# Reordering the list of batch 0, turning the last x by DMA, and moving one VectorE sum in a fused hash attention and gated feed-forward kernel

## The chip, the cores and the metric

The kernel runs on one core of a Trainium2 chip. A core has five engines that run their own instruction streams: TensorE (PE, matrix products; PEld is its weight load), VectorE (DVE), ScalarE (ACT), GpSimd (POOL) and SyncE (SP, which here issues most DMA transfers). The metric is the device time of one execution in microseconds (us); lower is better. Before the change the median of 3 runs is 340.48 us (340.46 to 341.31).

## What is computed

There are 4 batches, 8 heads, 768 positions and 64 values a head. First a masked attention: each query and each key gets a bucket of 6 sign bits, and a query sees the keys of its own bucket alone.

```python
q_bits = (einsum('bhsd,dk->bhsk', q, proj) > 0)      # the same for k
mask   = q_bucket[:, :, :, None] == k_bucket[:, :, None, :]
scores = where(mask, (q @ k^T) / sqrt(D), -1e9)
x      = softmax(scores) @ v                          # heads side by side: 3072 tokens x 512
```

Then a gated feed-forward block on x, with d_ff = 1536:

```python
ffn = (gelu(x @ w_gate) * (x @ w_val)) @ w_out
out = x + sigmoid(x @ w_res) * ffn
```

## The kernel before

A pair p is two heads; a batch has 4 pairs, and p runs from 0 to 15. The bits of queries and keys stand as extra rows beside the 64 values in a tile nat (token by column; four buffers, used in turn by pairs and sides), which is turned into aug (column by token), so that one matmul gives the masked score. The scores of a pair are cut into 9 chunks, so a batch has 36 slots: `scores` (line 542) makes 1024 columns in one of two PSUM buffers sp, ScalarE takes the exponential (line 553), and `values` (line 515) multiplies it with v (in the tile va, with a column of ones) into av. `finish` (lines 466 and 467) divides and writes x_tok; x_tok is turned into x_sb either by a DMA transpose that SP issues (line 470) or on TensorE (`x_turn`, lines 497 to 504: six transposes into PSUM and copies to SBUF).

`gate_val` (lines 570 to 588) then runs 12 steps m: 8 matmuls with w_gate, 8 with w_val (line 566), the Gelu on ScalarE (line 583), and their product hh on VectorE (line 586), which gives the sp buffer of w_val back. Behind the product of step m stand the pieces that were registered for it with `gv`. The last quarter of x is multiplied last in step 0: the first 12 matmuls (`begun`) are issued ahead. `project` (lines 592 to 623) is a generator that gives one matmul at a time; the matmuls of batch b's projection are dealt out over the 36 slots of batch b+1 by `mlp_mm`, and the last HELD = 16 of the 96 are kept to cover the turning of the last x.

The program's order is written out by hand; each engine runs its instructions in that order and waits on semaphores. For batch 0 it is the list ORDER (lines 20 to 30), names of pieces that `job` defines (lines 713 to 766). sN and vN are the scores and the values of slot N. trPS (P pair, S side: 0 query, 1 key) is VectorE's transpose for the hash, hNI a quarter of a hash product on TensorE, tkN its result back to tokens, btPS the bits, csPS the cast of the values into nat on GpSimd, tpPSH and tdPSH the turning of half H on TensorE and its copy on VectorE, tuPS the turning by DMA instead. ldPS and lvP are loads on SP, vaP and vsP the tile va and the sums of v on GpSimd, wN a piece of the weights loaded from GpSimd's queue (w0, w2, w4, w6: w_gate; w1, w3, w5, w7: w_val; w8: w_res; w9 to w11: w_out), finPH a finish, xtP an x_turn, g0 and g1 the begun matmuls, op40, pr40 and rp40 the preset of pair 4's result. The lists BESIDE (lines 31 to 44) say which pieces stand behind which step of batch 0's gate_val.

For the batches behind it, the bits of two of the pairs are made without TensorE: `part` (line 357, GpSimd) multiplies the values by one row of proj, and `part_sum` (line 361, VectorE) adds up; there are 24 of each a batch, and PROD and SUMS (lines 771 and 772) say behind which step each stands (12 and up are slots of the next batch). They are planned for batches 1 and 2.

Of the kernel before, what the change touches and what calls it, by code (L numbers as in the profile page):

```python
# [18 lines left out]
X_PE = 2  # L19
ORDER = """  # L20
trq tpB tdk tdq trk s0 hoq tr10 ld50 s1 bo0 s2 ho bo1 tp001 td001 s3 tp011 td011a ld40 tr11 ld51 v0
v1 cs21 td011b s4 s5 h00 h01 h02 h03 tr20 s6 s7 v2 v3 v4 tk0 bt10 bt11 tp100 tp110 td100 td110 tr21
s8 tr30 tr31 tp111 td111 cs31 s9 tp101 td101 s10 w0 v5 v6 v7 v8 s11 cs20 s12 ld61 fin00 ld41 h10 h11
w1 s13 h12 h13 fin01 cs30 s14 lv3 ld70 s15 va1 v9 v10 v11 s16 tk1 bt20 bt21 bt31 tp200 tp210 td200
td210 vs1 s17 tp211 td211 cs41 tr50 s18 tp201 td201 va2 s19 tp310 vs2 s20 vs3 bt30 td310 v12 v13 s21
v14 fin10 s22 tp300 tr40 w2 tp301 s23 v15 tr51 s24 lv4 va4 v16 v17 s25 v18 s26 v19 v20 v21 td301
td300 s27 fin11 v22 s28 cs50 tp311 s29 ld71 v23 fin20 w3 w4 s30 lv5 w5 v24 v25 td311 s31 v26 fin21
va3 tr41 v27 s32 w6 v28 v29 v30 s33 xt2 s34 v31 s35 gelu tr61 v32 v33 v34 g0 v35 fin30 op40 g1 fin31
xt3 ld60 h20 h21 h22 w7
"""  # L30
BESIDE = [
    "vs4 lv6 cs40 h23 tk2 bt41",
    "cs51 bt50",
    "tu50 cs70 tr70",
    "bt40 tu40 cs60 w8 w9 w10 w11",
    "bt51",
    "tr71",
    "tu51",
    "tr60",
    "h30 h31 h32 tu41 cs61 h33 tk3 bt60 bt61 tu60 tu61",  # L40
    "cs71 bt71 tu71",
    "bt70 tu70",
    "pr40 rp40",
]

@with_exitstack
def kernel(
# [13 lines left out]
    B, H, S, D = q.shape  # L61
# [7 lines left out]
    HP = H // 2  # L69
# [222 lines left out]
    def stripes(ht):  # L292
        n = ht.shape[1]
        return ht.rearrange("p (a c) n -> p a c n", a=3)[:, :, 0:HT // 3] if n > HT else \
            ht.rearrange("p (a c) n -> p a c n", a=3)
# [59 lines left out]
    def part(x, j):  # L355
        pd = t32_pool.tile([P, HT, D], FP32, tag="t32", name="pd")
        nc.gpsimd.tensor_mul(pd, raw[x], prow[:, j].unsqueeze(1).to_broadcast([P, HT, D]))  # L357
        hparts[x, j] = pd

    def part_sum(x, j):  # L360
        nc.vector.tensor_reduce(stripes(hsum6)[:, :, :, j],  # L361
                                hparts.pop((x, j)).rearrange("p (a c) d -> p a c d", a=3), axis=mybir.AxisListType.X, op=ALU.add)

    def bits_sum(x):
        nc.vector.tensor_scalar(nat_of(x)[:, :, D:D + NBITS].rearrange("p (a c) n -> p a c n", a=3),
                                stripes(hsum6), 0.0, 0.5,
                                op0=ALU.is_gt, op1=ALU.subtract)

    def turn(p, side):
        x = (p, side)  # L370
        ag = aug_pool.tile([P, HT, P], BF16, tag=f"aug{side}", name=f"aug{side}")
        nc.sync.dma_start_transpose(out=ag, in_=nat_of(x).rearrange("p c n -> p (c n)"))
        aug[x] = ag
# [84 lines left out]
    def finish(p, hi):  # L458
        b, hp = divmod(p, HP)
        if hp == 0 and hi == 0:  # L460
            x_tok[b] = x_pool.tile([P, HP, T, 2 * D], BF16, tag="x_tok", name="x_tok")
            x_sb[b] = x_pool.tile([P, HP, T, P], BF16, tag="x_sb", name="x_sb")
        o = av.pop((p, hi))
        acc_done((p, hi))
        rec = sm_pool.tile([P, T], FP32, tag="rec", name="rec")
        nc.vector.reciprocal(rec, o[:, 0:T, D])
        nc.vector.tensor_mul(x_tok[b][:, hp, :, hi * D:(hi + 1) * D], o[:, 0:T, 0:D],
                             rec.unsqueeze(2).to_broadcast([P, T, D]))
        if hi == 1 and (0 < b < B - 1 or hp < HP - (X_PE if b == 0 else 1)):
            nc.sync.dma_start_transpose(out=x_sb[b][:, hp],  # L470
                                        in_=x_tok[b][:, hp].rearrange("p t n -> p (t n)"))

# [23 lines left out]
    def x_turn(b, hp):  # L496
        pt = mm_ps.tile([P, T, P], BF16, tag=take(), name="pt")
        for t in range(T):
            nc.tensor.transpose(pt[:, t, :], x_tok[b][:, hp, t, :], ident)  # L499
        if hp == HP - 1:  # L500
            nc.scalar.activation(x_sb[b][:, hp, 0:2], pt[:, 0:2], AF.Copy)
            nc.vector.tensor_copy(x_sb[b][:, hp, 2:T], pt[:, 2:T])
        else:
            nc.vector.tensor_copy(x_sb[b][:, hp], pt)
# [154 lines left out]
    NSLOT = HP * NCH  # L659
    LAST = NPAIR * NCH  # L660
    LAG = 2
    HELD = 16
    AHEAD = 3
    side_pe, side_work = {}, {}

# [103 lines left out]

    FROM = 1  # L770
    PROD = (0, 0, 0, 0, 0, 1, 2, 2, 6, 7, 8, 8, 10, 10, 10, 12, 13, 13, 13, 19, 19, 20, 22, 27)
    SUMS = (1, 2, 2, 4, 5, 6, 7, 8, 9, 10, 10, 11, 12, 12, 13, 17, 19, 21, 21, 23, 23, 29, 30, 31)
    PROD0 = (0, 1, 2, 3, 4, 5, 6, 7, 8, 9, 10, 11, 12, 14, 16, 17, 19, 20, 22, 24, 25, 27, 28, 30)
    SUMS0 = (1, 2, 3, 4, 5, 6, 7, 8, 9, 10, 11, 12, 14, 16, 18, 19, 21, 22, 24, 26, 27, 29, 30, 32)
    CASTS0 = (3, 5, 8, 10)
    CASTS = (2, 5, 10, 11)
    VALS = (9, 6)
    LAYS = (0, 0, 3, 5)
# [4 lines left out]
    for b in range(B - 1):  # L783
        s0, p0 = b * NSLOT, (b + 1) * HP
        xs = [(p0 + i, side) for i in range(2) for side in range(2)]
        ys = [(p0 + 2 + i, side) for i in range(2) for side in range(2)]
        if b > 0:
            for j, (x, y) in enumerate(zip(xs, ys)):
                at(s0 + 24 + 2 * j, lambda x=x: tr(*x))
                at(s0 + 25 + 2 * j, lambda x=x: cast(*x, nc.gpsimd))  # L790
                loads(s0 + 2 + 4 * j, (x[0], "qk"[x[1]]))
                loads(s0 + 18 + 3 * j, (y[0], "qk"[y[1]]))
            gv(b, 0, lambda p0=p0: tokens((p0, p0 + 1), True))
            for m, x in zip(LAYS, xs):
                lay(b, m, x)
            for m, y in zip(CASTS, ys):
                gv(b, m, lambda y=y: cast(*y, nc.gpsimd))
        else:
            for m, names in enumerate(BESIDE):
                for name in names.split():  # L800
                    gv(b, m, first.pop(name))
        if b >= FROM:
            s1 = s0 + NSLOT

            def put(n, piece):
                if n < 0:
                    at(s1 + n, piece)
                elif n < KF:
                    gv(b, n, piece)
                else:  # L810
                    at(s1 + n - KF, piece)

            plan, prod, sums = [], PROD if b else PROD0, SUMS if b else SUMS0
            for i, (y, j) in enumerate((y, j) for y in ys for j in range(NBITS)):
                plan.append((prod[i] + .3, lambda y=y, j=j: part(y, j)))
                plan.append((sums[i] + .2, lambda y=y, j=j: part_sum(y, j)))
                if j == NBITS - 1:
                    plan.append((sums[i] + .2, lambda y=y: (bits_sum(y), turn(*y))))
            for n, piece in sorted(plan, key=lambda e: e[0]):
                put(int(n // 1), piece)  # L820
    for p in range(HP, NPAIR):
# [6 lines left out]
    mlp, done = [], [0]  # L828
    NMM = T * (KM + KF)

    def mlp_mm(n):
        while mlp and n > 0:
            try:
                next(mlp[0])
                n -= 1
                done[0] += 1
            except StopIteration:
                mlp.pop(0)
# [6 lines left out]
    for s in range(NSLOT, LAST):  # L845
        p, c = divmod(s, NCH)
        b, slot = divmod(s, NSLOT)
        cur = scores(p, c)
        for piece in side_pe.pop(s, []):
            piece()  # L850
        mlp_mm(AHEAD + (slot + 1) * (NMM - HELD - AHEAD) // NSLOT - done[0])
        pending.append(cur)
        while len(pending) > LAG:
            values(*pending.pop(0))
        for piece in side_work.pop(s, []):
            piece()
        if slot == NSLOT - 1:
            values(*pending.pop(0))
            ps = (HP * (b + 1), HP * (b + 1) + 1)
            mlp_mm(4)  # L860
            flush()
            begun = [gv_mm(b, 0, w, 0, KM - 1) for w in (wg, wv)]
            if b < B - 1:
                mlp_mm(NMM)
                gate_val(b, begun, lambda: hashed(ps))
            else:
                x_turn(b, HP - 1)
                mlp_mm(HELD - 7)
                gv(b, 0, lambda: mlp_mm(NMM))
                gate_val(b, begun, lambda: mlp_mm(3))  # L870
            done[0] = 0
            mlp.append(project(b))
# [33 lines left out]
```

## Time and profile before

| what | value |
|---|---|
| median of 3 runs | 340.48 us |
| profiled execution | 340.31 us |
| its span, first to last instruction | 338.6 us |
| TensorE busy | 333.2 us (98%) |
| VectorE busy | 216.9 us (64%) |
| ScalarE busy | 206.2 us (61%) |
| GpSimd busy | 171.9 us (51%) |
| granted TensorE clock | 1.000 |

The list of batch 0 reaches its first gate matmuls at 44.38 us; its gate_val ends at 79.9. Each later batch then has its 36 slots and its gate_val: the first score of batch 1 stands at 79.93, that of batch 2 at 158.50, that of batch 3 at 237.07. A row of a timeline reads: start, duration, engine, line, operation, what it writes and reads, shapes, count, and in brackets the idle time of the engine just before it and what ended it. Matmuls are pipelined, so a row's duration holds the latency of the last one; the distance between the starts of two rows is what they take. SPq and POOLq rows are the issue of a DMA; its landing is a number of its own.

### The profile page before, as it was taken

To read this page: it belongs to the slowest core of one execution; us is meant where nothing else is said; L and a number is where in the kernel's file an instruction comes from. 1 tells how busy PE (TensorE), PEld (TensorE's weight loads), DVE (VectorE), ACT (ScalarE), POOL (GpSimd) and SP (SyncE) were. 2 spreads that over 40 slices of the span, in tenths; PEclk is the share of its full clock that TensorE was granted. 3 is DMA by queue.
4 is the path that set the end of the run, shared out by engine and by line. 5 is a ranking of instruction groups with operands and counts; after the bars stand their busy time and mean duration, and the time that the engine had idled before them with its cause. 6 is when DMAs were issued, how large, how long until landed. Compare 5 with 4: busy or idle time off the path is not lost.

```text
span 338.6 us, 7598 instructions
## 1 busy us (share of the span) xinstructions
PE 333.2 (98%) x3058; PEld 203.1 (60%) x3058; DVE 216.9 (64%) x418; ACT 206.2 (61%) x232; POOL 171.9 (51%) x220
## 2 busy tenths in 40 slices
PE   8999999999999999999999999999999999999995
PEld 4667766655666655655666665656566665666444
DVE  6889457574445748888887766887897444343343
ACT  4889963317999952235999982233999984223220
POOL 5879920410665306998999704998998000000000
PEclk9999999999999999999999999999999999999999
DMA  7997897799876634350488832551261420000012
GB/s 211 379 249 169 160 252 128 132 190 199 240 164 187 207 94 99 73 96 0 126 219 204 277 106 62 102 96 28 48 148 39 97 56 33 31 0 2 31 64 94
DMA packets 71459, 43.09 MB, mean 127 GB/s; under 512 B 49536, under 2 KB 68480, under 8 KB 71424
## 3 DMA queue, kind: packets, MB, share of 16 engines
q1 hardware_dynamic: 65008, 37.37, 43.7%
q0 software_dynamic: 6336, 5.24, 10.1%
q8 instruction: 24, 0.39, 0.5%
q14 instruction: 11, 0.09, 0.1%
q10 hardware_dynamic: 80, 0.00, 0.0%
HBM read 29.56 MB, written 6.29 MB: 106 GB/s over the span
## 4 chain that ended last, share of the span: by engine, by line
PE 91%; ACT 4%; DVE 3%; issue 1%; DVEq 0%; ACTq 0%
PE sp L566 35%; PE fps L614 18%; PE sp L542 17%; PE av L515 9%; PE rps L598 6%; ACT hh L553 4%; PE hs L283 2%; DVE hh L586 1%; PE wps L189 1%; PE pt L384 1%; PE hs L330 1%; DVE nat L319 1%; DVE hsum L361 0%; PE pt L499 0%; DVE o L621 0%
## 5 line engine op out<-in xcount | busy, mean ns | idle before, releaser
L553 ACT ACTIVATE e<-sp 128x1024 bf16<-128x1024 f32 x108 | 109.0, 1028 | 8.1 <-PE sp L542 2.8
L357 POOL TENSOR_TENSOR pd<-ld,prow 128x768 f32<-128x768 f32 x48 | 86.1, 1811 | 36.8 <-PE hs L283 32.6
L583 ACT ACTIVATE gt<-sp 128x768 bf16<-128x768 f32 x48 | 38.9, 810 | 89.8 <-PE sp L566 89.8
L542 PE MATMUL sp<-aug,aug 71*128 71x256 bf16 (+1 forms) x384 | 85.5, 325 | 0.1
L614 PE MATMUL fps<-wo,hh 128*128 128x512 bf16 (+2 forms) x312 | 79.5, 362 | 0.0
L566 PE MATMUL sp<-x_sb,wv 128*128 128x512 bf16 (+1 forms) x384 | 70.9, 326 | 0.4 <-DVE hh L586 0.4
L566 PE MATMUL sp<-x_sb,wg 128*128 128x512 bf16 (+1 forms) x384 | 70.9, 326 | 0.1
L586 DVE TENSOR_TENSOR hh<-gt,sp 128x768 bf16<-128x768 bf16 x48 | 45.8, 954 | 39.0 <-PE sp L566 34.2
L515 PEld LDWEIGHTS <-e 128*128 128x128 bf16 x864 | 40.2, 97 | 25.1
L566 PEld LDWEIGHTS <-wv 128*128 128x128 bf16 x384 | 37.6, 98 | 25.5 <-issue 0.8
L566 PEld LDWEIGHTS <-wg 128*128 128x128 bf16 x384 | 36.9, 98 | 25.8 <-issue 1.7
L361 DVE TENSOR_REDUCE hsum<-pd 128x12 f32<-128x768 f32 x48 | 44.4, 943 | 0.5
L515 PE MATMUL av<-va,e 128*128 128x65 bf16 x864 | 43.4, 193 | 0.0
L614 PEld LDWEIGHTS <-hh 128*128 128x128 bf16 x312 | 28.1, 97 | 21.8
L553 ACT ACTIVATE hh<-sp 128x1024 bf16<-128x1024 f32 x36 | 34.5, 1024 | 3.4 <-PE sp L542 3.0
L542 PEld LDWEIGHTS <-aug 71*128 71x128 bf16 x384 | 29.5, 97 | 11.0 <-issue 1.1
L617 DVE SCALAR_TENSOR_TENSOR fps<-th,fps 128x512 f32<-128x512 f32 (+2 forms) x26 | 16.9, 650 | 28.3 <-PE fps L614 27.8
L598 PE MATMUL rps<-wr,x_sb 128*128 128x512 bf16 x96 | 27.1, 379 | 0.0
L494 DVE COPY av<-av 128x390 f32<-128x390 f32 x24 | 13.7, 571 | 19.6 <-PE av L490 19.6
L602 ACT ACTIVATE th<-rps 128x512 f32<-128x512 f32 x24 | 14.3, 594 | 18.5 <-PE rps L598 18.5
L223 POOL TENSOR_SCALAR nat<-ld 128x768 bf16<-128x768 f32 (+1 forms) x16 | 13.0, 813 | 18.6 <-DMA aug<-nat 18.0
L265 DVE STREAM_TRANSPOSE t<-ld 128x768 f32<-128x768 f32 (+1 forms) x24 | 21.9, 925 | 0.1
(77 smaller groups left out, 259.6 us busy)
## 6 DMA issues: line engine op xcount, KB each, us to landing
ldv<-in_v_dram SPq DMA_DIRECT2D x16, 384.0 KB, 5.1
out_dram<-o SPq DMA_DIRECT2D x23, 256.0 KB, 2.0
ld<-in_q_dram SPq DMA_DIRECT2D x15, 384.0 KB, 5.6
ld<-in_k_dram SPq DMA_DIRECT2D x15, 384.0 KB, 6.0
wg<-in_moe_w_gate_dram POOLq DMA_DIRECT2D x4, 384.0 KB, 9.1
wv<-in_moe_w_val_dram POOLq DMA_DIRECT2D x4, 384.0 KB, 11.8
wo<-in_moe_w_out_dram POOLq DMA_DIRECT2D x3, 512.0 KB, 11.8
wr<-in_moe_w_res_dram POOLq DMA_DIRECT2D x1, 512.0 KB, 7.7
```

What stands on the lines that cost most here:

```text
L265: nc.vector.transpose(t32[p, side][:, sl].rearrange("p c h n -> p (c h n)"), raw[p, side][:, sl].rearrange("p c d -> p (c d)"))
L357: nc.gpsimd.tensor_mul(pd, raw[x], prow[:, j].unsqueeze(1).to_broadcast([P, HT, D]))
L361: nc.vector.tensor_reduce(stripes(hsum6)[:, :, :, j], hparts.pop((x, j)).rearrange("p (a c) d -> p a c d", a=3), axis=mybir.AxisListType.X ...
L515: nc.tensor.matmul(av[p, hi][:, qt, :], e[:, off:off + P], va[:, hi, jt, 0:D + 1], start=first, stop=(p >= HP and jt == T - 1), skip_group ...
L542: nc.tensor.matmul(sp[:, off:off + nq * P], ks[0:KA, hi * T + jt, :], qs[0:KA, hi * T + qt0:hi * T + qt0 + nq, :], start=True, stop=True)
L553: nc.scalar.activation(e, sp, AF.Exp, scale=float(ALPHA))
L566: nc.tensor.matmul(sp[:, c0:c1], w[:, kk, bass.ts(m, P)], xs[:, kk, c0:c1], start=(kk == 0), stop=(kk == KM - 1))
L583: nc.scalar.activation(gt, sp[:, 0:S], AF.Gelu)
L586: nc.vector.tensor_mul(hidden[b][:, m, :], gt, ps[1][:, 0:S])
L598: nc.tensor.matmul(rps, x_sb[b][:, kk, t, :], wr[:, kk, :], start=(kk == 0), stop=(kk == KM - 1))
L614: nc.tensor.matmul(fps[:, cs], hh[:, m, bass.ts(t, P)], wo[:, m, cs], start=(m == 0), stop=(m == KF - 1))
L617: nc.vector.scalar_tensor_tensor(fps[:, cs], th[:, cs], 1.0, fps[:, cs], op0=ALU.add, op1=ALU.mult)
```

## The change

The first 27 names of the list stand as they are. Behind them the same pieces stand in another order; some loads, casts and weight pieces move far, and some pieces change between the list and the steps of gate_val (w8 comes into the list; w6, w7 and the others stand together at its end). BESIDE is dealt out anew: w8 leaves, the hash of pairs 6 and 7 goes from step 8 to step 9, tr70 from 2 to 3, tr60 from 7 to 4.

The fifth entry of SUMS goes from 5 to 4, in batches 1 and 2. PROD0, SUMS0 and CASTS0 go; nothing read them, because the loop plans these pieces from batch 1 on.

In the last batch the fourth pair's x is turned by a DMA transpose like the others, and `x_turn` is not called there any more. Four more matmuls of the projection are held back in that batch, from slot 12 on one by one up to 20 instead of 16, and of them 10 instead of 9 stand between the begun matmuls and the last quarter of step 0.

```diff
 ORDER = """
 trq tpB tdk tdq trk s0 hoq tr10 ld50 s1 bo0 s2 ho bo1 tp001 td001 s3 tp011 td011a ld40 tr11 ld51 v0
-v1 cs21 td011b s4 s5 h00 h01 h02 h03 tr20 s6 s7 v2 v3 v4 tk0 bt10 bt11 tp100 tp110 td100 td110 tr21
-s8 tr30 tr31 tp111 td111 cs31 s9 tp101 td101 s10 w0 v5 v6 v7 v8 s11 cs20 s12 ld61 fin00 ld41 h10 h11
-w1 s13 h12 h13 fin01 cs30 s14 lv3 ld70 s15 va1 v9 v10 v11 s16 tk1 bt20 bt21 bt31 tp200 tp210 td200
-td210 vs1 s17 tp211 td211 cs41 tr50 s18 tp201 td201 va2 s19 tp310 vs2 s20 vs3 bt30 td310 v12 v13 s21
-v14 fin10 s22 tp300 tr40 w2 tp301 s23 v15 tr51 s24 lv4 va4 v16 v17 s25 v18 s26 v19 v20 v21 td301
-td300 s27 fin11 v22 s28 cs50 tp311 s29 ld71 v23 fin20 w3 w4 s30 lv5 w5 v24 v25 td311 s31 v26 fin21
-va3 tr41 v27 s32 w6 v28 v29 v30 s33 xt2 s34 v31 s35 gelu tr61 v32 v33 v34 g0 v35 fin30 op40 g1 fin31
-xt3 ld60 h20 h21 h22 w7
+v1 cs21 td011b s4 tr20 s5 h00 h01 h02 h03 tk0 bt10 bt11 s6 v2 v3 v4 cs20 s7 tp100 td100 tp110 td110
+tr30 s8 tp111 td111 v5 s9 tp101 cs31 tr21 tr31 s10 v6 v7 v8 s11 w0 w1 td101 s12 vs1 fin00 h10 h11
+s13 fin01 ld61 h12 va1 h13 s14 ld41 s15 v9 v10 v11 s16 lv4 tk1 bt20 bt21 bt31 tp200 tp210 td200 cs30
+ld70 td210 s17 tr40 tp211 td211 tr50 vs2 s18 tp201 s19 tp310 td310 s20 td201 cs41 va2 w2 v12 v13 s21
+v14 s22 bt30 tp300 s23 tr51 lv3 vs3 td300 v15 v16 s24 fin10 tp301 td301 s25 v17 v18 fin11 s26 v19
+v20 v21 s27 tp311 tr61 s28 v22 v23 fin20 s29 va3 cs50 v24 v25 s30 td311 v26 s31 v27 v28 va4 fin21
+s32 v29 v30 s33 lv5 v31 fin30 s34 xt2 ld71 ld60 op40 tr41 v32 v33 s35 v34 g0 v35 fin31 gelu g1 xt3
+w3 w4 w5 w6 w7 w8 h20 h21 h22
 """
 BESIDE = [
-    "vs4 lv6 cs40 h23 tk2 bt41",
-    "cs51 bt50",
-    "tu50 cs70 tr70",
-    "bt40 tu40 cs60 w8 w9 w10 w11",
-    "bt51",
+    "cs40 h23 tk2 bt50",
+    "bt40 tu40 cs51",
+    "tu50 cs70 bt51",
+    "vs4 bt41 tr70 cs60",
+    "w9 w10 w11 tr60",
+    "",
+    "lv6",
     "tr71",
-    "tu51",
-    "tr60",
-    "h30 h31 h32 tu41 cs61 h33 tk3 bt60 bt61 tu60 tu61",
-    "cs71 bt71 tu71",
-    "bt70 tu70",
-    "pr40 rp40",
+    "tu41 cs61",
+    "tu51 cs71 h30 h31 h32 h33 tk3 bt60 bt61 tu60",
+    "tu61 bt70 bt71 tu71",
+    "pr40 rp40 tu70",
 ]
...
-        if hi == 1 and (0 < b < B - 1 or hp < HP - (X_PE if b == 0 else 1)):
+        if hi == 1 and (b > 0 or hp < HP - X_PE):
...
+    HELD_LAST = 20
...
-    SUMS = (1, 2, 2, 4, 5, 6, 7, 8, 9, 10, 10, 11, 12, 12, 13, 17, 19, 21, 21, 23, 23, 29, 30, 31)
+    SUMS = (1, 2, 2, 4, 4, 6, 7, 8, 9, 10, 10, 11, 12, 12, 13, 17, 19, 21, 21, 23, 23, 29, 30, 31)
...
-        mlp_mm(AHEAD + (slot + 1) * (NMM - HELD - AHEAD) // NSLOT - done[0])
+        held_back = (HELD_LAST - HELD) * (b == B - 1) * max(0, slot - 12) // (NSLOT - 1 - 12)
+        mlp_mm(AHEAD + (slot + 1) * (NMM - HELD - AHEAD) // NSLOT - held_back - done[0])
...
-                x_turn(b, HP - 1)
-                mlp_mm(HELD - 7)
+                mlp_mm(HELD_LAST - 10)
                 gv(b, 0, lambda: mlp_mm(NMM))
                 gate_val(b, begun, lambda: mlp_mm(3))
```

More of the change, by code (lines that the diff above doesn't have):

```diff
@@ L771 @@
     PROD = (0, 0, 0, 0, 0, 1, 2, 2, 6, 7, 8, 8, 10, 10, 10, 12, 13, 13, 13, 19, 19, 20, 22, 27)
-    SUMS = (1, 2, 2, 4, 5, 6, 7, 8, 9, 10, 10, 11, 12, 12, 13, 17, 19, 21, 21, 23, 23, 29, 30, 31)
-    PROD0 = (0, 1, 2, 3, 4, 5, 6, 7, 8, 9, 10, 11, 12, 14, 16, 17, 19, 20, 22, 24, 25, 27, 28, 30)
-    SUMS0 = (1, 2, 3, 4, 5, 6, 7, 8, 9, 10, 11, 12, 14, 16, 18, 19, 21, 22, 24, 26, 27, 29, 30, 32)
-    CASTS0 = (3, 5, 8, 10)
+    SUMS = (1, 2, 2, 4, 4, 6, 7, 8, 9, 10, 10, 11, 12, 12, 13, 17, 19, 21, 21, 23, 23, 29, 30, 31)
     CASTS = (2, 5, 10, 11)
@@ L811, in put @@
                     at(s1 + n - KF, piece)
-            plan, prod, sums = [], PROD if b else PROD0, SUMS if b else SUMS0
+            plan = []
             for i, (y, j) in enumerate((y, j) for y in ys for j in range(NBITS)):
-                plan.append((prod[i] + .3, lambda y=y, j=j: part(y, j)))
-                plan.append((sums[i] + .2, lambda y=y, j=j: part_sum(y, j)))
+                plan.append((PROD[i] + .3, lambda y=y, j=j: part(y, j)))
+                plan.append((SUMS[i] + .2, lambda y=y, j=j: part_sum(y, j)))
                 if j == NBITS - 1:
-                    plan.append((sums[i] + .2, lambda y=y: (bits_sum(y), turn(*y))))
+                    plan.append((SUMS[i] + .2, lambda y=y: (bits_sum(y), turn(*y))))
             for n, piece in sorted(plan, key=lambda e: e[0]):
```

## The prediction

> **What bounds the kernel now.** I read the page's busy shares first, then the timelines of the engines in the three stretches that the change touches, then the DMA issues with their times to landing. The profiled execution took 340.31 us (a span of 338.6 and 1.71 around it); the median of the runs is 340.48. The sum below is made against 340.31, and 0.17 is added at the end.
>
> ```profile
> PE 333.2 (98%) x3058; PEld 203.1 (60%) x3058; DVE 216.9 (64%) x418; ACT 206.2 (61%) x232; POOL 171.9 (51%) x220
> ```
>
> TensorE looks full everywhere, but matmul ends are modelled, so a matmul that stands in the queue counts as busy. What it does not show is in the list of batch 0. Timeline of ScalarE (start, duration, idle before and what ended it):
>
> ```profile
> 17.46 2.85 ACT L553 ACTIVATE hh<-sp 128x1024 bf16<-128x1024 f32 x3 [0.73 <-PE sp L542]
> 20.80 2.86 ACT L553 ACTIVATE hh<-sp 128x1024 bf16<-128x1024 f32 x3 [0.49 <-PE sp L542]
> 23.90 21.09 ACT L553 ACTIVATE hh<-sp 128x1024 bf16<-128x1024 f32 x22 [0.24 <-PE sp L542]
> 45.00 1.28 ACT L764 ACT_TABLE_LOAD   x1
> ```
>
> From 23.90 on, 22 exponentials stand back to back, one each 0.956 us ((21.09 - 1.02) / 21): there ScalarE sets the pace, and before it the exponentials still wait for scores. All behind 27 pieces that can be gained at the front is those gaps, 0.73 + 0.49 + 0.24 = 1.46 us. From the end of the list on TensorE is dense, and each delay of it stays.
>
> **The list, -0.34.** Up to s6 TensorE does the same work at the same times. s7 then comes 0.9 later, behind v2 to v4, but s8's exponential still begins at 17.46: in both orders TensorE reaches s8 only behind tp110, which waits for the last bits of pair 1. Then the orders part. TensorE before:
>
> ```profile
> 18.96 1.14 PE L515 MATMUL av<-va,hh 128*128 128x65 bf16 x32
> ...
> 20.11 1.03 PE L542 MATMUL sp<-aug,aug 71*128 71x512 bf16 x5
> 21.07 0.86 PE L283 MATMUL hs<-t,projw 128*32 128x192 f32 x16
> 21.88 0.59 PE L542 MATMUL sp<-aug,aug 71*128 71x256 bf16 x3
> ```
>
> v5 (8 of the 32 value matmuls, 0.24) moves ahead of s9, where TensorE would wait for the copies td100 and td110. s9 then ends about 0.2 later, which ScalarE hardly feels, and v6 to v8 end at 19.96 instead of 20.11. s11 starts there, s12 when a buffer is free (20.42), h10 and h11 (0.80) at 20.86, s13 at 21.65, h12 and h13 at 22.08, s14 at 22.87; its exponential starts at 23.52, when the one before it ends, instead of 23.90. The VectorE transposes for these hashes (tr30, td111, tr21, tr31) end at 20.80 in the new order, just in time. From 23.52 the exponentials run on at 0.956 if no gap of TensorE's own pieces exceeds some 0.8 us between two score groups (0.956 less 0.43 for the scores, plus the little that the second buffer lends). I went through the new order: the fullest places are v19 v20 v21 (0.73) and xt2 v32 v33 (0.82), which may cost 0.1 together. At the end the chain is the same as before (last exponential, v35, its finish, xt3, the hash, the last quarter of the first gate), so of 0.38 I take 0.34. Ends: 1.46 gained, and the loss of the second rival below.
>
> On SP the transpose of x_sb for pair 0 now stands ahead of the loads ld61 and ld41, and lv4 and ld70 ahead of lv3; what that can cost is rival 2. lv3 takes the buffer that va1 leaves at 23, is issued at about 27 and lands by 33; vs3 and va3 (2.1 and 0.8 on POOL) end at 36, and v27 reads them at 39.5. On POOL the weight pieces w3 to w7 go behind va4, from 36.5 to 40.4 before to some 38 to 42. The slowest took this long to land:
>
> ```profile
> wv<-in_moe_w_val_dram POOLq DMA_DIRECT2D x1, 384.0 KB, 15.3
> ```
>
> So the last is there by 58, and it is read at about 70, in step 9: cost nothing, covered by nine steps of gate and value products of 2.6 each.
>
> **The pieces beside gate and value of batch 0, +0.38.** VectorE must end each step's product hh within 0.02 us of its normal time, or TensorE waits. In step 3 it now has bt41 and tr70 behind hh (before: bt40 alone). Their price, from VectorE's timeline (and from the list a transpose with what follows it):
>
> ```profile
> 60.43 0.95 DVE L586 TENSOR_TENSOR hh<-gt,sp 128x768 bf16<-128x768 bf16 x1 [0.80 <-PE sp L566]
> 61.41 0.98 DVE L319 TENSOR_SCALAR nat<-htp 32x72 bf16<-32x72 f32 x4
> ```
> ```profile
> 27.66 0.98 DVE L265 STREAM_TRANSPOSE t<-ld 128x768 f32<-128x768 f32 x1
> 28.57 0.51 DVE L393 COPY aug<-pt 71x768 bf16<-71x768 bf16 x1
> ```
>
> hh to bits 0.98, the bits 1.01 (143.80 to 144.81 below), a transpose 0.91: 2.90 against a step of 2.60, so +0.30 (ends: 0, and the transpose's whole 0.91). tk3 with bt60 and bt61 moves from step 8 to 9 together with its hash matmuls, which give VectorE the room as before: 0. In step 10 bt70 and bt71 together (0.98 + 2 x 0.98 + 0.03) put the last hh 0.37 late:
>
> ```profile
> 80.17 0.95 DVE L586 TENSOR_TENSOR hh<-gt,sp 128x768 bf16<-128x768 bf16 x1 [0.66 <-PE av L490]
> ```
> ```profile
> 81.45 0.60 PE L542 MATMUL sp<-aug,aug 71*128 71x256 bf16 x3
> ```
>
> It would end at 81.49, and its buffer is wanted by the score at 81.45: with the semaphore +0.08; the rest is covered by one score and five projection matmuls. The DMA transposes tu60 to tu71 go out some 2.6 later, with over 10 us before pair 6 reads them: 0. The earlier w8 costs nothing (wr is read after this stage).
>
> **The fifth sum, -0.74.** Batch 1; VectorE, TensorE, then GpSimd:
>
> ```profile
> 135.01 0.95 DVE L586 TENSOR_TENSOR hh<-gt,sp 128x768 bf16<-128x768 bf16 x1 [0.78 <-PE sp L566]
> 135.88 1.81 DVE L361 TENSOR_REDUCE hsum<-pd 128x12 f32<-128x768 f32 x2
> 137.61 0.95 DVE L586 TENSOR_TENSOR hh<-gt,sp 128x768 bf16<-128x768 bf16 x1
> ...
> 143.80 0.98 DVE L319 TENSOR_SCALAR nat<-htp 32x72 bf16<-32x72 f32 x4
> 144.81 0.95 DVE L361 TENSOR_REDUCE hsum<-pd 128x12 f32<-128x768 f32 x1
> ```
> ```profile
> 143.84 1.46 PE L566 MATMUL sp<-x_sb,wv 128*128 128x512 bf16 x8
> 145.14 1.46 PE L566 MATMUL sp<-x_sb,wg 128*128 128x512 bf16 x8
> 146.81 1.46 PE L566 MATMUL sp<-x_sb,wv 128*128 128x512 bf16 x8 [0.20 <-DVE hh L586]
> ```
> ```profile
> 137.53 3.57 POOL L357 TENSOR_TENSOR pd<-ld,prow 128x768 f32<-128x768 f32 x2
> ```
>
> Eight matmuls start 1.30 after the eight before them; here it is 1.67, so 0.37 is lost behind bits and a sum in step 5. The sum moves to step 4, as its second. Two sums behind one hh just fit: 135.01 to 137.61 is 2.60. Its product is the first of the two at 137.53, done by 139.4, and the sum would start at 141.95. So 0.37 in each of batches 1 and 2 (ends: 0 and 0.37 each; what comes late next is nothing, since hh and bits alone take 1.99).
>
> **The last x, -0.43.** Six transposes and a wait for the Gelu leave TensorE (batch 3):
>
> ```profile
> 281.87 0.50 PE L499 MATMUL pt<-ident,x_tok 128*128 128x128 bf16 x6
> 282.21 2.11 PE L614 MATMUL fps<-wo,hh 128*128 128x512 bf16 x9
> ...
> 285.54 1.46 PE L566 MATMUL sp<-x_sb,wg 128*128 128x512 bf16 x8
> ```
>
> 0.34 is the transposes; 0.09 the wait: the three matmuls ahead of 285.54 end at 285.45. Two copies (0.38 on ScalarE, 0.42 on VectorE) go too, off the path. The four more matmuls that are held back are only moved: a slot of 1.19 (42.9 us over 36) loses under 0.04 each and stays above the exponential's 0.956. What the DMA transpose must hide behind is 12 gate matmuls (1.95) and 10 projection matmuls (10 x 0.216): 4.11 us. Batch 1 does it that way already (TensorE, SP, the time to landing of that one, and of the slowest in batches 1 to 3, issued with loads in flight):
>
> ```profile
> 122.81 1.14 PE L566 MATMUL sp<-x_sb,wg 128*128 128x512 bf16 x6
> ```
> ```profile
> 123.82 1.22 SPq L470 DMA_TRANSPOSE x_sb<-x_tok  x1
> ```
> ```profile
> DMA to landing us min/median/max: 2.7/2.7/2.7
> ```
> ```profile
> DMA to landing us min/median/max: 4.5/4.5/4.5
> ```
>
> It lands 123.82 + 2.7 - 122.81 = 3.71 after the gate begins; 0.40 is left. On SP the write of the last but one tile now stands behind the transpose; nothing waits for it. Ends: -0.43, and +0.97 with a landing of 4.5. What speaks against the edit at all is rival 3.
>
> **Sum.** 340.31 - 0.34 + 0.38 - 0.74 - 0.43 = 339.18; on the scale of the median of the runs, + 0.17, 339.3 us.
>
> **Rivals.** (1) The list gives nothing: a copy or product comes late in the new order, and the first gate starts when it did. For it: several of my times above agree within 0.1 us. Against: the gaps before 23.90 are TensorE's, and its work there gets less. With the other terms 339.65. (2) Slower: cs41 on POOL must wait for ld41, and va2, vs3 and va3 stand behind it. SP and the landings (of loads issued at 25.54 and at 37.45):
>
> ```profile
> 22.62 2.20 SPq L470 DMA_TRANSPOSE x_sb<-x_tok  x1
> ```
> ```profile
> ld<-in_q_dram SPq DMA_DIRECT2D x1, 384.0 KB, 5.5
> ```
> ```profile
> ld<-in_q_dram SPq DMA_DIRECT2D x1, 384.0 KB, 9.8
> ```
> ```profile
> 29.09 0.83 POOL L432 CAST va<-ldv 128x768 bf16<-128x768 f32 x1
> ```
>
> ld41 is issued at about 25.5, behind that transpose and ld61. At 5.5 it lands at 31.0, and cast, va2 and its ones are done at 32.8; v18 wants va2 at 34.0 (23.52 + 9 x 0.956 + 1.02, a score 0.43, v17 0.41). From a landing of 32.2 on each us costs one: at 9.8 us it lands at 35.3, 3.1 lost, 342.4. Against it: two loads fewer are in flight between 12.7 and 22. (3) The transpose should have stayed on TensorE: the landing of the last x takes 4.5 us, as one did with loads beside it; the gate begins 1.40 late (1.01 + 4.5 - 4.11), so the stretch loses 0.97 instead of gaining 0.43: 340.7. Against: no load is in flight then, and two of its kind landed in 2.7. The Trainium skill, "VectorE: DVE Perf Modes", section "Rules for kernel authors", sides with this rival: a 128x128 transpose belongs on TensorE where PSUM will do as its target, and on the DMA otherwise. Its section "The three transpose paths" gives 390 ns and 1309 ns for a block; six blocks by DMA one behind the other would be an estimate of 7.9 us, and the sum by it 344. The trace disagrees on the size: six blocks landed in 2.7 us. (4) The change does not do what it says: VectorE's extra work in steps 3 and 10 takes a whole transpose (0.91) and the front gains nothing: 340.31 + 0.17 + 0.91 + 0.08 - 0.74 - 0.43 = 340.3. (5) More of the gaps close, say 0.6 us more: 338.7.
>
> **How the numbers follow.** This kernel's runs tell about 0.3% (1.0 us) from no change. Chances: the forecast 0.45 (its own range 339.0 to 339.7, about three quarters of it under 339.46), rival 1 0.16, 2 0.14, 3 0.07, 4 0.08, 5 0.10. Faster by over 0.3%: 0.34 + 0.10 and a little of rival 1, 0.45. Slower: rival 2 where the landing takes over 9 us, 0.13. Within: 0.42. The range goes from 338.5 (rival 5) to 340.8 (rivals 3 and 4) and leaves out rival 2.
>
> **What would show it.** The long run of exponentials starts near 23.5 and stays unbroken (list); the fourth to fifth hh of batch 0's gate stand 2.9 apart, and TensorE waits about 0.3 there; no wait for hh in batches 1 and 2, where 1.67 becomes 1.30; no transposes at line 499 in batch 3 and no idle TensorE before the last quarter of its first gate. Wrong would make it: a gap in ScalarE between 33 and 36 behind va2, or a product beside which a load or copy runs that I put at its old time.

## The result

The changed kernel takes 339.86 us (median of 17 runs, 339.18 to 340.29); the kernel before 340.90 (17 runs, 340.18 to 342.03). The ratio is 0.9966, with an interval of 0.9957 to 0.9976: 0.34% faster, just over what can be told from no change. The profiled execution took 339.51 us, and its span fell from 338.6 to 337.7.

Busy shares say as little as before. Page of the changed kernel:

```profile
PE 330.1 (98%) x3005; PEld 202.3 (60%) x3052; DVE 216.3 (64%) x417; ACT 205.9 (61%) x231; POOL 171.9 (51%) x220
```

(Some matmul records are missing in it.) What tells is the distance between fixed points of TensorE's timeline: A from the first exponential to the last quarter of the first gate, B from there to the first score of batch 1, C from there to that of batch 2, D to that of batch 3, E to the gate matmuls of step 1 in batch 3, F to the first matmul of the last residual projection; the last column is what is left to the end of the span. All values are us, from one profiled execution each; the lower rows are the experiments below.

| kernel | first exponential | A list | B gate 0 | C batch 1 | D batch 2 | E batch 3, last x | F | A to F | F to end |
|---|---|---|---|---|---|---|---|---|---|
| before | 7.80 | 40.57 | 31.56 | 78.57 | 78.57 | 48.47 | 45.86 | 323.60 | 7.20 |
| changed | 7.81 | 40.38 | 31.91 | 78.32 | 78.21 | 48.06 | 45.87 | 322.75 | 7.12 |
| sum_back | 7.89 | 40.37 | 31.91 | 78.68 | 78.57 | 48.07 | 45.86 | 323.46 | 7.12 |
| x_on_pe | 8.50 | 40.37 | 31.91 | 78.32 | 78.21 | 48.47 | 45.86 | 323.14 | 7.19 |
| short_cover | 7.61 | 40.38 | 31.92 | 78.32 | 78.21 | 48.62 | 45.86 | 323.31 | 7.13 |
| spread_beside | 7.70 | 40.37 | 31.57 | 79.64 | 78.22 | 48.06 | 45.86 | 323.72 | 7.12 |
| v5_back | 7.66 | 40.41 | 31.91 | 78.32 | 78.21 | 48.06 | 45.87 | 322.78 | 7.16 |
| v32_v33_back | 8.34 | 40.37 | 31.91 | 78.32 | 78.21 | 48.06 | 45.87 | 322.74 | 7.14 |
| beside_refit | 7.82 | 40.37 | 33.28 | 78.66 | 78.22 | 48.06 | 45.86 | 324.45 | 7.15 |
| list_alone | 8.05 | 40.37 | 31.91 | 78.68 | 78.58 | 48.46 | 45.86 | 323.86 | 7.19 |
| no_list | 7.72 | 40.57 | 31.57 | 78.34 | 78.20 | 48.06 | 45.86 | 322.60 | 7.66 |
| refit_two | 8.38 | 40.45 | 31.57 | 78.21 | 78.21 | 48.06 | 45.87 | 322.37 | 7.55 |
| refit_three | 7.68 | 40.37 | 31.57 | 78.21 | 78.21 | 48.06 | 45.87 | 322.29 | 7.68 |

A stretch that an edit does not touch comes back within about 0.02, with one exception (C of no_list, below). The last column is 7.12 to 7.20 in ten runs, but 7.55 to 7.68 in no_list, refit_two and refit_three: there SP issues the last output DMA 4.65 to 4.67 behind F instead of 4.42, and it lands 1.71 to 1.84 after its issue instead of 1.53 to 1.57. Why is open, so A to F of these three does not tell their time to the end.

The list gained 0.19, the pieces beside gate 0 cost 0.35 in B and 0.11 at the start of C, the fifth sum gave 0.36 in each of C and D, the last x 0.41: -0.85 in all up to F.

The rows behind it follow the order of the kernel. **List.** ScalarE of the changed kernel (start, duration, idle before and what ended it):

```profile
16.14 1.02 ACT L553 ACTIVATE hh<-sp 128x1024 bf16<-128x1024 f32 x1 [0.31 <-PE sp L542]
17.47 3.01 ACT L553 ACTIVATE hh<-sp 128x1024 bf16<-128x1024 f32 x3 [0.31 <-PE sp L542]
20.66 2.92 ACT L553 ACTIVATE hh<-sp 128x1024 bf16<-128x1024 f32 x3 [0.17 <-PE sp L542]
23.88 20.01 ACT L553 ACTIVATE hh<-sp 128x1024 bf16<-128x1024 f32 x21 [0.30 <-PE sp L542]
44.06 1.02 ACT L553 ACTIVATE hh<-sp 128x1024 bf16<-128x1024 f32 x1 [0.17 <-PE sp L542]
```

The long run starts at 23.88 as before (23.90), not at 23.52, and the last exponential stands at 44.06. TensorE in front of that run, and at the end of the list:

```profile
19.96 1.16 PE L542 MATMUL sp<-aug,aug 71*128 71x512 bf16 x5
21.05 0.86 PE L283 MATMUL hs<-t,projw 128*32 128x192 f32 x16
21.84 0.61 PE L542 MATMUL sp<-aug,aug 71*128 71x256 bf16 x3
22.38 0.86 PE L283 MATMUL hs<-t,projw 128*32 128x192 f32 x16
23.17 1.04 PE L542 MATMUL sp<-aug,aug 71*128 71x512 bf16 x5
...
41.20 0.60 PE L542 MATMUL sp<-aug,aug 71*128 71x512 bf16 x2
...
43.36 0.60 PE L542 MATMUL sp<-aug,aug 71*128 71x512 bf16 x3
43.95 0.42 PE L515 MATMUL av<-va,hh 128*128 128x65 bf16 x8
44.20 1.14 PE L566 MATMUL sp<-x_sb,wg 128*128 128x512 bf16 x6
...
48.19 0.50 PE L566 MATMUL sp<-x_sb,wg 128*128 128x512 bf16 x2
```

**Gate of batch 0.** VectorE, then TensorE, of the changed kernel: two products 2.97 apart with the bits and tr70 between them, and w_val matmuls 1.65 behind the gate's:

```profile
57.65 0.95 DVE L586 TENSOR_TENSOR hh<-gt,sp 128x768 bf16<-128x768 bf16 x1 [0.63 <-PE sp L566]
58.63 0.95 DVE L319 TENSOR_SCALAR nat<-htp 32x72 bf16<-32x72 f32 x4
59.61 0.98 DVE L265 STREAM_TRANSPOSE t<-ld 128x768 f32<-128x768 f32 x1
60.62 0.95 DVE L586 TENSOR_TENSOR hh<-gt,sp 128x768 bf16<-128x768 bf16 x1
```
```profile
59.98 1.46 PE L566 MATMUL sp<-x_sb,wg 128*128 128x512 bf16 x8
61.63 1.46 PE L566 MATMUL sp<-x_sb,wv 128*128 128x512 bf16 x8 [0.19 <-DVE hh L586]
```

**Fifth sum.** Two sums behind one hh, then the bits alone, and no wait (VectorE, TensorE):

```profile
141.36 1.81 DVE L361 TENSOR_REDUCE hsum<-pd 128x12 f32<-128x768 f32 x2
143.09 0.95 DVE L586 TENSOR_TENSOR hh<-gt,sp 128x768 bf16<-128x768 bf16 x1
144.08 0.98 DVE L319 TENSOR_SCALAR nat<-htp 32x72 bf16<-32x72 f32 x4
145.69 0.95 DVE L586 TENSOR_TENSOR hh<-gt,sp 128x768 bf16<-128x768 bf16 x1 [0.63 <-PE sp L566]
```
```profile
144.12 1.46 PE L566 MATMUL sp<-x_sb,wv 128*128 128x512 bf16 x8
145.42 1.46 PE L566 MATMUL sp<-x_sb,wg 128*128 128x512 bf16 x8
146.72 1.46 PE L566 MATMUL sp<-x_sb,wv 128*128 128x512 bf16 x7
```

**Last x.** SP, the time to landing, TensorE:

```profile
279.66 1.22 SPq L470 DMA_TRANSPOSE x_sb<-x_tok  x1
```
```profile
DMA to landing us min/median/max: 2.8/2.8/2.8
```
```profile
281.45 1.46 PE L614 MATMUL fps<-wo,hh 128*128 128x512 bf16 x5
282.75 0.49 PE L566 MATMUL sp<-x_sb,wg 128*128 128x512 bf16 x2
283.07 0.49 PE L566 MATMUL sp<-x_sb,wv 128*128 128x512 bf16 x2
283.40 1.46 PE L614 MATMUL fps<-wo,hh 128*128 128x512 bf16 x6
284.69 1.46 PE L566 MATMUL sp<-x_sb,wg 128*128 128x512 bf16 x8
```

The transpose lands at 282.46, and TensorE wants it at 282.75.

### The profile page after: what moved, and what is told of

Its sections match the earlier page's. It is cut to its first block, busy times and chain, and to the rows that moved or that the text cites. A ratio compares the mean times of both kernels' runs of the same rounds, so it can differ in the third digit from the quotient of the medians.

```text
span 337.7 us, 7536 instructions
## 1 busy us (share of the span) xinstructions
PE 330.1 (98%) x3005; PEld 202.3 (60%) x3052; DVE 216.3 (64%) x417; ACT 205.9 (61%) x231; POOL 171.9 (51%) x220
## 4 chain that ended last, share of the span: by engine, by line
PE 95%; DVE 2%; issue 1%; ACT 0%; DVEq 0%
PE sp L566 36%; PE sp L542 19%; PE fps L614 18%; PE av L515 10%; PE rps L598 6%; PE hs L283 2%; PE pt L384 2%; PE wps L189 1%; PE hs L330 1%; DVE hh L586 1%; DVE o L621 1%; DVE fps L617 0%; PE av L487 0%; DVE nat L319 0%; ACT gt L583 0%
## 5 line engine op out<-in xcount | busy, mean ns | idle before, releaser
L614 PE MATMUL fps<-wo,hh 128*128 128x512 bf16 (+2 forms) x289 | 75.0, 361 | 1.3
L566 PE MATMUL sp<-x_sb,wv 128*128 128x256 bf16 (+1 forms) x376 | 70.5, 325 | 0.6 <-DVE hh L586 0.2
L566 PE MATMUL sp<-x_sb,wg 128*128 128x256 bf16 (+1 forms) x376 | 70.5, 325 | 0.5
L515 PEld LDWEIGHTS <-e 128*128 128x128 bf16 x864 | 40.2, 97 | 25.0
L598 PE MATMUL rps<-wr,x_sb 128*128 128x512 bf16 x88 | 25.2, 379 | 0.3
```

What stands on the lines that cost most here:

```text
L515: nc.tensor.matmul(av[p, hi][:, qt, :], e[:, off:off + P], va[:, hi, jt, 0:D + 1], start=first, stop=(p >= HP and jt == T - 1), skip_group ...
L566: nc.tensor.matmul(sp[:, c0:c1], w[:, kk, bass.ts(m, P)], xs[:, kk, c0:c1], start=(kk == 0), stop=(kk == KM - 1))
L598: nc.tensor.matmul(rps, x_sb[b][:, kk, t, :], wr[:, kk, :], start=(kk == 0), stop=(kk == KM - 1))
L614: nc.tensor.matmul(fps[:, cs], hh[:, m, bass.ts(t, P)], wo[:, m, cs], start=(m == 0), stop=(m == KF - 1))
```

## The experiments

**The fifth sum back.**

```diff
-    SUMS = (1, 2, 2, 4, 4, 6, ...
+    SUMS = (1, 2, 2, 4, 5, 6, ...
```

> The changed kernel with the fifth entry of SUMS at 5 again, nothing else. My theory: the sum stands behind the bits of step 5 again and holds back the product that the next step's value matmuls wait for; the stretch from step 5's to step 6's w_val matmuls grows from 1.30 + 1.30 to 2.97, so 0.36 in batch 1 and 0.36 in batch 2, and the span from 337.7 to 338.4. Rival: the sum's lateness is absorbed by the rest of the changed kernel (the changed step order gives each later step some slack), and the time per batch stays within 0.1.

C grew by 0.36, D by 0.36, and nothing else moved. TensorE of this run, where the changed kernel has 1.30 between the starts:

```profile
145.49 1.46 PE L566 MATMUL sp<-x_sb,wg 128*128 128x512 bf16 x8
147.15 1.03 PE L566 MATMUL sp<-x_sb,wv 128*128 128x512 bf16 x5 [0.20 <-DVE hh L586]
```

The rival, that the sum's lateness is absorbed, is out.

**The last x on TensorE again.**

```diff
-        if hi == 1 and (b > 0 or hp < HP - X_PE):
+        if hi == 1 and (0 < b < B - 1 or hp < HP - (X_PE if b == 0 else 1)):
...
-    HELD_LAST = 20
+    HELD_LAST = 16
...
-                mlp_mm(HELD_LAST - 10)
+                x_turn(b, HP - 1)
+                mlp_mm(HELD - 7)
```

> The changed kernel with the last x turned on TensorE again (six transposes, two copies, 16 held matmuls). My theory: the stretch from the first score of batch 3 to the second step's gate matmuls grows from 48.06 to 48.47 (0.34 of transposes and 0.07 of a wait for the Gelu), the span to 338.1. Rival 3, weakened by the result already: the DMA's landing costs as much as the transposes, and the stretch stays within 0.1 of 48.06. The Trainium skill, "VectorE: DVE Perf Modes", section "Rules for kernel authors", has a 128x128 transpose on TensorE where PSUM will do; by it this kernel would be the faster of the two.

E went back to 48.47, so the DMA transpose is worth 0.41 here. By the rule of the Trainium skill ("VectorE: DVE Perf Modes", section "Rules for kernel authors"), a 128x128 transpose on TensorE where PSUM will do, this kernel would have been the faster one. The run decides against it at this place: TensorE is the engine that is short here, and the DMA lies behind work that has to be done anyway.

**A shorter cover.**

```diff
-                mlp_mm(HELD_LAST - 10)
+                mlp_mm(HELD_LAST - 14)
```

> The changed kernel with 6 instead of 10 projection matmuls between the begun gate matmuls of batch 3 and the last quarter of its first gate; the four go behind that quarter. My theory: the transpose lands at about 282.46, 0.29 before TensorE wants it in the changed kernel; with 0.86 of cover taken away TensorE waits 0.5 to 0.6 for it, and the end is 0.5 later (span 338.2). Rival: the transfer is hidden anyway (TensorE's wait ends on something else, or the four matmuls fill a wait for the Gelu further on that is there already), under 0.15.

E grew by 0.56. TensorE of this run:

```profile
281.26 0.59 PE L614 MATMUL fps<-wo,hh 128*128 128x512 bf16 x2
282.25 0.49 PE L566 MATMUL sp<-x_sb,wg 128*128 128x512 bf16 x2 [0.40 <-DMA x_sb<-x_tok]
```

The wait now ends on the transpose. Of the 0.86 of cover taken away (4 x 0.216), 0.30 was spare. The landing is on the edge of the path, not deep behind it.

**tr70 and bt71 elsewhere beside gate 0.**

```diff
-    "vs4 bt41 tr70 cs60",
+    "vs4 bt41 cs60",
...
-    "",
+    "tr70",
...
-    "tu61 bt70 bt71 tu71",
-    "pr40 rp40 tu70",
+    "tu61 bt70",
+    "pr40 rp40 tu70 bt71 tu71",
```

> The changed kernel with the transpose tr70 behind step 5 of batch 0's gate, which has no piece, instead of behind step 3, and the bits bt71 with their transposes by DMA behind step 11 instead of step 10. My theory: the 0.35 lost in step 4 and the 0.10 before the first score of batch 1 were VectorE's extra 0.9 behind one product; the distance from the last quarter of the first gate to the first score of batch 1 falls from 31.91 to 31.5, the span to 337.25. Rival: the loss has another cause (w_val or a value cast arriving late), and the stretch stays at 31.9, or it moves to step 6, where tr70 meets the load lv6, or into the first slots of batch 1, where bt71 is now late.

Half of each side came true. B fell to 31.57: tr70 behind step 3 was the whole 0.34. But C rose by 1.32. TensorE, then VectorE, at the start of batch 1:

```profile
80.08 1.03 PE L598 MATMUL rps<-wr,x_sb 128*128 128x512 bf16 x4
82.37 0.38 PE L614 MATMUL fps<-wo,hh 128*128 128x512 bf16 x1 [1.26 <-DVE nat L319]
```
```profile
80.75 0.56 DVE L494 COPY av<-av 128x390 f32<-128x390 f32 x1
81.33 0.98 DVE L319 TENSOR_SCALAR nat<-htp 32x72 bf16<-32x72 f32 x4
```

The projection's first tile fps comes from the same PSUM pool as htp (lines 610 and 300), and its matmul waits until bt71, htp's last reader, is done. The changed kernel has bt71 behind step 10, where it costs 0.11. A piece that looks free to wait can hold a buffer.

**v5 back behind s10.**

```diff
-tr30 s8 tp111 td111 v5 s9 tp101 cs31 tr21 tr31 s10 v6 v7 v8 ...
+tr30 s8 tp111 td111 s9 tp101 cs31 tr21 tr31 s10 v5 v6 v7 v8 ...
```

> The changed kernel with v5 behind s10 again, nothing else. Measured from the first exponential, so that the opening's scatter falls out; the last quarter of the first gate then stands at 40.38 in the changed kernel and at 40.57 before. My theory: v5 ahead of s9 makes s9 0.24 late, ScalarE loses 0.16 between its 9th and 11th exponential, and the buffer that s12 waits for comes that much later, so that the front's gain is eaten; with v5 back the long run of exponentials starts 0.2 to 0.3 earlier (23.6 to 23.7 on the changed kernel's scale) and, as ScalarE now sets the end of the list, the last quarter of the first gate 0.2 to 0.3 earlier: 40.1 to 40.2. Rival: the hash matmuls and copies of pair 1 set the start of the long run whatever s9 does, and both stay as in the changed kernel.

My theory fell: A is 40.41, not 40.1 to 40.2. ScalarE of this run, whose first exponential stands at 7.66:

```profile
17.32 2.85 ACT L553 ACTIVATE hh<-sp 128x1024 bf16<-128x1024 f32 x3 [0.30 <-PE sp L542]
20.67 2.85 ACT L553 ACTIVATE hh<-sp 128x1024 bf16<-128x1024 f32 x3 [0.49 <-PE sp L542]
23.76 4.84 ACT L553 ACTIVATE hh<-sp 128x1024 bf16<-128x1024 f32 x5 [0.24 <-PE sp L542]
```

s9's lateness is gone (2.85 instead of 3.01), but the next wait takes what it gave (0.49 instead of 0.17), and s14's exponential stands 16.10 behind the first, where the changed kernel has 16.07 and the kernel before 16.10. With v5 ahead of s8 (refit_two, below) it is 16.15. The place of v5 is worth less than 0.1.

**v32 and v33 back behind s35.**

```diff
-... tr41 v32 v33 s35 v34 g0 v35 ...
+... tr41 s35 v32 v33 v34 g0 v35 ...
```

> The changed kernel with v32 and v33 behind s35 again, as before the change. If the 0.19 gained up to the last quarter of the first gate came from these two having moved ahead of s35, it is lost again: 40.57 from the first exponential. My theory is that they move beside idle TensorE only: the gap of 0.17 before the last exponential goes, v34 still waits for the exponential of s34, and the quarter stays at 40.4 (within 0.05); the 0.19 then comes from TensorE being less far behind at s33 (its score began at 41.20 instead of 41.44).

A stays at 40.37: moving these two gained nothing. The starts of the exponentials of s26 to s35, counted from the first, show where the two kernels part:

```
before   27.46 28.47 29.39 30.29 31.19 32.10 33.16 34.33 35.25 36.15
changed  27.43 28.60 29.52 30.46 31.39 32.31 33.21 34.12 35.02 36.25
```

Up to s26 the new list has gained 0.03. Before, s32 and s33 come 1.06 and 1.17 behind the exponential ahead of them; in the changed kernel the wide step is at s27, and s32 to s34 follow at 0.90. TensorE before, at s33:

```profile
40.70 0.90 PE L515 MATMUL av<-va,hh 128*128 128x65 bf16 x24
41.44 0.60 PE L542 MATMUL sp<-aug,aug 71*128 71x512 bf16 x2
```

There s33 stands behind v28 to v30 and begins at 41.44; now it stands behind v29 and v30 alone and begins at 41.20. So s34's exponential is 0.23 earlier, v34 follows it, and g0 follows v34: 44.20 instead of 44.38. From g0 to the last quarter both kernels take 3.99. This is read off the two traces; no run moves v28 alone.

**The list alone.** The kernel before, with the new ORDER and BESIDE (their diff stands in the change) and no other edit.

> The kernel before with the new list and its pieces beside the gate, and nothing else of the change. If the parts add: first exponential to the last quarter of the first gate 40.38 (-0.19), from there to the first score of batch 1 31.91 (+0.35), to that of batch 2 78.68 (+0.11), the rest as before; together 0.27 slower than before. Rival: the list also feeds the later parts (earlier loads), and part of the 0.77 of the fifth sum and the last x belongs to it; then the stretches of batches 1 to 3 come out shorter than before.

The parts add to 0.02: -0.20, +0.35, +0.11, and the rest as before. By itself the new list, with its pieces beside gate 0, makes the kernel 0.26 slower. The rival, that the list feeds the later parts, is out.

**The hash of pairs 6 and 7 as before the change.**

```diff
-    "vs4 bt41 tr70 cs60",
+    "vs4 bt41 cs60",
...
-    "",
+    "tr70",
...
-    "tu41 cs61",
-    "tu51 cs71 h30 h31 h32 h33 tk3 bt60 bt61 tu60",
-    "tu61 bt70 bt71 tu71",
+    "tu41 cs61 h30 h31 h32 h33 tk3 bt60 bt61 tu60",
+    "tu51 cs71 tu61 bt71 tu71",
+    "bt70",
```

> The changed kernel with tr70 behind step 5, and the hash of pairs 6 and 7 with its bits spread over steps 8, 9 and 10 as before the change, so that bt71 is done before the first projection matmul of batch 1, which takes over the PSUM buffer that bt71 reads. My theory: both losses of batch 0's gate are gone without the 1.26 of the run that had bt71 behind step 11; from the last quarter of the first gate to the first score of batch 1 31.57, from there to the first score of batch 2 78.21 instead of 78.32; span 337.25 at the changed kernel's opening. Rival: the order of the transposes by DMA (tu61 and tu71 now a step earlier) or tr70 behind step 5 makes a new wait, and the two stretches together stay at 110.2.

Slower by 1.70: the rival's new wait came, and larger than it said. VectorE and SP of this run:

```profile
74.80 0.95 DVE L586 TENSOR_TENSOR hh<-gt,sp 128x768 bf16<-128x768 bf16 x1 [0.21 <-PE sp L566]
79.45 0.99 DVE L319 TENSOR_SCALAR nat<-htp 32x72 bf16<-32x72 f32 x4 [3.70 <-DMA aug<-nat]
80.47 0.95 DVE L586 TENSOR_TENSOR hh<-gt,sp 128x768 bf16<-128x768 bf16 x1
```
```profile
73.76 8.27 SPq L372 DMA_TRANSPOSE aug<-nat  x4
```

bt71 writes the nat buffer that tu51 must have left. I had put tu51 behind tu60 on SP; tu60 waits for its bits and is issued at 73.76, tu51 after it at 75.25, and it lands some 4 us later. VectorE's product stands behind bt71, and TensorE behind the product.

**The same with tu51 ahead, and v5 ahead of s8.** Step 3 loses tr70, steps 5 to 11 read as below, and the list has `tr30 v5 s8 tp111 td111 s9`.

```diff
+    "tr70",
+    "lv6 tu51",
+    "tr71",
+    "tu41 cs61 h30 h31 h32 h33 tk3 bt60 bt61 tu60 tu61",
+    "cs71 bt71 tu71",
+    "bt70 tu70",
+    "pr40 rp40",
```

> The changed kernel with three things moved. (a) v5 ahead of s8, where TensorE waits 0.21 for a copy, instead of ahead of s9. (b) tr70 behind step 5 instead of step 3. (c) The hash of pairs 6 and 7 and its bits behind steps 8, 9 and 10 as before the change, and this time the transpose tu51 behind step 6, so that on SP it is not queued behind tu60, which waits for bits. By my reading the stretches are: first exponential to the last quarter of the first gate 40.2 to 40.25 (from 40.38; if the front is held by something else than s9's lateness, 40.38 to 40.42 as with v5 back); from there to the first score of batch 1 31.57 (from 31.91); from there to batch 2 78.21 (from 78.32); the rest as in the changed kernel. Sum from the first exponential 322.15 to 322.3 against 322.75, and 1.3 to 1.45 less than before: about 0.996 of the kernel before by the median. Rival: SP's order was not the cause of the loss with the refitted steps, and bits in steps 8 or 9 wait again: the gate stretch above 32.

B and C are 31.57 and 78.21: SP's order was the cause. A is 40.45, 0.07 worse, so v5 ahead of s8 is no gain either. Median 339.68 (10 runs, 339.37 to 340.17), ratio to the kernel before 0.9966 (0.9953 to 0.9978).

**Without the list.** The changed kernel with the old ORDER and BESIDE.

> The changed kernel with the list and the pieces beside the gate as before the change: only the fifth sum and the last x are new. If the parts add, the stretches are 40.57, 31.56, 78.21, 78.21, 48.06 and 45.86, the sum from the first exponential 322.47, 0.28 less than the changed kernel. Rival: the loads and casts of the old list come too late or the parts depend on one another, and the sum is 322.75 or more.

322.60 up to F: 0.15 less than the changed kernel, and 0.13 over my sum. The 0.13 comes in at one place, the preset of pair 5 (line 490). TensorE, then GpSimd, of this run:

```profile
90.28 0.60 PE L542 MATMUL sp<-aug,aug 71*128 71x512 bf16 x2
90.84 0.19 PE L490 MATMUL av<-vsum,eps_sb 128*128 128x65 bf16 x1
```
```profile
90.68 0.10 POOL L444 MEMSET vsum<- 128x2 bf16 x1
```

In the kernel before, the preset follows 0.43 behind the start of these scores; here it stands 0.56 behind, because the last write of vsum, which it reads, ends only 0.05 ahead of it. GpSimd's chain starts with a copy (line 353) that waits for a small load; it begins at 87.83 here, at 87.32 before the change and at 82.27 in the changed kernel. Up to this place the run has the same instructions as the kernel before, which has no such wait, so the 0.13 belongs to one execution's late load, not to the parts: the parts add. The new list brings that load some 5 us earlier.

**Only the pieces beside gate 0 refitted.** As refit_two, with v5 left ahead of s9.

> The changed kernel with only the pieces beside batch 0's gate refitted (tr70 behind step 5, tu51 behind step 6, the hash of pairs 6 and 7 and its bits behind steps 8 to 10), v5 left ahead of s9. If the stretches add: 40.38, 31.57, 78.21, 78.21, 48.06, 45.86, sum from the first exponential 322.29, 0.46 less than the changed kernel and 1.31 less than before; by the median 0.9955 to 0.996 of the kernel before. Rival: with v5 ahead of s9 the earlier hash collides with something and the sum stays above 322.4.

The sum up to F is 322.29, as worked out: 0.46 less than the changed kernel, 1.31 less than before. The median is 339.95 (10 runs, 339.33 to 340.32) and the ratio 0.9961 (0.9945 to 0.9976). To the end nothing is gained over the changed kernel: the profiled spans are 337.64 and 337.68, since the opening is 0.13 earlier and what follows F 0.56 longer, and the lowest times are 339.33 and 339.18. The refit is shown for B and C, not for the whole kernel.

## Why the prediction was right, and where it was not

Forecast 339.3, measured 339.86; against a kernel before of 340.48 by the first three runs and 340.90 by all 17. As a difference: -1.13 forecast, -0.85 in the stretches up to F, -0.92 in the profiled spans, -1.04 in the medians. The sign and the size hold. That the list gained at all is luck in part: it gained almost all of it at its end, where the forecast saw nothing. The list with its pieces alone would have been a loss of 0.26 (list_alone); the gain is that of the sum and of the last x.

- **The list, -0.34: measured -0.19, and by another way.** Two steps failed. The first is "which ScalarE hardly feels": s9's lateness moved s10's exponential, whose buffer s12 waits for, so s12 began at 20.53 (17.47 + 3.01 = 20.48, and the semaphore) instead of 20.42. I had also left out some 0.1 between a score and the hash matmuls behind it, twice: 21.84 + 0.43 is 22.27, and they start at 22.38. From s11 (19.96, as forecast) to s14 (23.17 instead of 22.87) this used up the gain, and v5_back and refit_two show that another place for v5 does not bring it back. The second is "At the end the chain is the same as before": it took the end as following the front, but the row of 22 exponentials hid two late starts, s32 and s33, behind TensorE's values, and there the new order gained. What would shorten the front stays open.
- **Pieces beside gate 0, +0.38: measured +0.46**, 0.35 for step 3 (forecast 0.30; the products were 2.97 apart, not 2.90) and 0.11 for step 10 (forecast 0.08). The mechanism held: spread_beside and refit_three give both back.
- **The fifth sum, -0.74: measured -0.72**, and sum_back takes it away again.
- **The last x, -0.43: measured -0.41.** The margin was 0.40 in the forecast, 0.30 by short_cover; the landing took 2.8 instead of 2.7.
- **Rivals.** Of rival 2 the wait was there, the price not. GpSimd of the changed kernel:

```profile
30.76 0.82 POOL L225 CAST nat<-ld 128x768 bf16<-128x768 f32 x1 [1.58 <-DMA ld<-in_k_dram]
```

 The cast cs41 waited for ld41 until 30.76 (forecast 31.0), and va2 was there before v18 wanted it. For the front of the list (23.88 against 23.90 before) rival 1 was closer than my forecast; its time, though, should read 339.7 (339.18 + 0.34 + 0.17). Rival 3 is refuted by x_on_pe, rival 4 by B, which lost 0.35 and not 0.91 (and A gained); rival 5 did not come.

## What to carry to other kernels

When an engine's idle time is to be gained by reordering another's work, walk the new order instruction by instruction and count the small gaps that the old trace shows at the same kinds of border. A row of n instructions with a good mean can hide two late starts, so print their starts. Before a piece is called free to wait, ask which buffer it holds, who takes that buffer next, and what stands ahead of its transfer on the queue that issues it: bt71 and tu51 cost 1.3 and 1.7 us in that way. A comparison by stretches has to run to the end of the span: the refits' 0.46 was gone there.

## What was not expected

The opening varies more than the whole change is worth, while what stands behind it repeats to 0.02 up to F, but for the 0.13 of no_list. The first exponential stands between 7.61 and 8.50 over the 13 profiled executions. TensorE's first hash matmuls show where that comes from; the changed kernel, then x_on_pe, which has the same instructions up to there:

```profile
4.28 1.67 PE L330 MATMUL hs<-t,projs 128*128 128x192 f32 x8
```
```profile
4.29 2.43 PE L330 MATMUL hs<-t,projs 128*128 128x192 f32 x8
```

They start together, but in x_on_pe single matmuls start 0.32 apart up to 6.03 and 0.16 apart behind that; in the changed kernel they start 0.16 apart from 4.65 on. Over all 13 executions the eight take 1.54 to 2.46: in the four where they take 1.54 the first exponential stands at 7.61 to 7.70, in the two where they take 2.43 and 2.46 at 8.50 and 8.38. So the opening is late where TensorE comes late to its quicker pace. What makes it come late was not looked into.

Single times follow the opening: x_on_pe took 340.53 us, more than the profiled execution of the kernel before (340.31), though its stretches sum to 0.46 less, because its opening was 0.70 later. Counting from a fixed point behind the opening makes one execution enough for differences of some 0.2 us, and for smaller ones where several runs agree.
